# Fourteen small loads of 2 to 15 rows into an unread scratch tile, in a decode step of attention beside a dense layer

## The chip, the cores and the metric

The kernel runs on one core of a Trainium2 chip. The metric is the device time of one execution in microseconds. Before the change it is 189.0 us, the median of three runs (188.88 to 189.22). One further execution was profiled, and all times by line or by engine come from it.

## What is computed

One token for each of two sequences. The layer-normed row goes through attention over the last 4096 positions of a key and value cache, with 16 query heads on 8 cached heads of 256 values, and beside it through a dense layer with the mish activation. Both are added to the input.

```
def reference(A_x, A_k_cache, A_v_cache, A_wq, A_wo, B_x, B_w1, B_b1, B_w2):
    ...
        W = min(4096, max(256, Sk // 4))
        q = (x @ wq).reshape(B, Sq, Hq, Dh).transpose(0, 2, 1, 3)
        k = jnp.repeat(k_cache[:, :, Sk - W:, :], rep, axis=1)
        v = jnp.repeat(v_cache[:, :, Sk - W:, :], rep, axis=1)
        scores = jnp.einsum("bhqd,bhkd->bhqk", q, k) * (Dh ** -0.5)
        p = _softmax(scores, axis=-1)
        o = jnp.einsum("bhqk,bhkd->bhqd", p, v)
        return o.transpose(0, 2, 1, 3).reshape(B, Sq, Hq * Dh) @ wo
    ...
        h = jnp.einsum("bsd,df->bsf", x, w1) + b1
        sp = jnp.log1p(jnp.exp(-jnp.abs(h))) + jnp.where(h > 0, h, jnp.zeros_like(h))
        act = h * jnp.tanh(sp)
        return jnp.einsum("bsf,fd->bsd", act, w2)

    x = A_x
    xn = _layernorm(x, axis=-1)
    return x + _A_ref(xn, A_k_cache, A_v_cache, A_wq, A_wo) + _B_ref(xn, B_w1, B_b1, B_w2)
```

All inputs are bfloat16. Of the caches only the last 4096 of 32768 positions are read.

## The kernel before

Every input byte is used once, so the kernel is a stream of loads with the work arranged around it. All large loads are issued by SyncE (SP) on one queue. They go to 128 partitions.

The work is cut into four units `u` of two cached heads for both sequences. For each unit there are two K tiles of 4 MB (`load_k`, L94), two V tiles of 4 MB (`load_v`, L100) and 0.9 MB of the output weight (`load_wo`, L109). K tiles, V tiles, the query weight and the two dense weights share a ring of three 4 MB buffers (`ring`, L89), so a load waits until the buffer's earlier tile has been consumed. The wo tiles have two buffers of their own.

For a unit, VectorE transposes a K tile (`turns`, L266), TensorE forms the scores (`scores`, L340), ScalarE takes the exponential, VectorE transposes the weights, and TensorE multiplies them with V (`values`, L394). `gather`, `finish`, `relay` and `mix_early` bring the result of the unit through its part of the output weight into one sum in PSUM.

The order on every engine is the order in which the program is written; nothing is reordered by a scheduler. Before the loop the program issues the query weight in two halves, the first two K tiles, b1 (two rows, L129) and w1 (L500). The loop over the first three units issues, at its top, the loads

```
        load_k(u + 1, 0)
        load_v(u, 0)
        load_k(u + 1, 1)
        load_v(u, 1)
        load_wo(u)
```

and then the computation. SP executes these in order, so an issue behind a waiting one waits too. After the loop come the loads of the last unit: a V tile (L613), 2.5 MB of the second V tile (L614), its wo part, the rest of that V tile in pieces of 1 and 0.5 MB (L616, L617), and w2 in four parts (L549) of 784, 448, 224 and 112 KB. The small matmuls of `pace` (L569) write a PSUM tile that is not read. The last matmuls are those of `mix` and `dense_out` (L560), which add the last wo and w2 parts to the sum `acc`; two copies into `res` and a store of its two rows (L649) end the program.

The tile `act_bf` (L496) and the constants are in the pool `consts`, which has one buffer for each tile.

Of the kernel before, what the change touches and what calls it, by code (L numbers as in the profile page):

```python
# [11 lines left out]
BF16 = mybir.dt.bfloat16  # L12
# [5 lines left out]
def kernel(  # L18
# [13 lines left out]
    nc = tc.nc  # L32
# [42 lines left out]
    consts = ctx.enter_context(tc.tile_pool(name="consts", bufs=1))  # L75
# [13 lines left out]
    def ring(name):  # L89
        return kv_pool.tile([P, RK * KE], BF16, tag="kv", name=name)  # L90
# [3 lines left out]
    def load_k(u, r):  # L94
        t = ring("k")
        src = kview[u][:, s0:, :].rearrange("j (c t) d -> c j (t d)", c=C)
        nc.sync.dma_start(out=t[:], in_=src[:, :, r * RK * KE : (r + 1) * RK * KE])
        k_t[u, r] = t

    def load_v(u, g, lo=0, hi=TV):  # L100
        if lo == 0:
            v_t[u, g] = ring("v")
        t = v_t[u, g]
        src = vview[u][:, s0:, :].rearrange("j (g x t) d -> g x j (t d)", g=GV, x=C)
        nc.sync.dma_start(
            out=t[:, lo * Dh : hi * Dh], in_=src[g, :, :, lo * Dh : hi * Dh]
        )

    def load_wo(u):  # L109
        w = wo_pool.tile([P, KU, rep, 2 * D], BF16, tag="wo", name="wo")  # L110
        nc.sync.dma_start(
            out=w[:].rearrange("p k h e -> p (k h e)"),
            in_=A_wo.rearrange("(k u y i) d -> u y k (i d)", k=KU, u=U, i=8)[u],
        )
        wo_t[u] = w
# [8 lines left out]
    for lo in (0, half):  # L124
# [14 lines left out]
        out=halves[:], in_=ident[0:2, 0:2].unsqueeze(2).to_broadcast([2, 2, Bsz])  # L139
# [5 lines left out]
    for k in range(KU):  # L145
        nc.gpsimd.tensor_copy(
            out=hot[:, k, :, :, :, k],
            in_=ident[:].rearrange("p (q y) -> p y q", y=4).unsqueeze(2)
# [11 lines left out]
        out=rstd[:], in_=mv[:, 1:2], func=ACT.Sqrt, bias=eps_t[:], scale=1.0  # L160
# [4 lines left out]
        out=xn_bf[:],  # L165
# [8 lines left out]
        out=parm[:], in_=ident[:].rearrange("p (a o) -> p o a", o=2), axis=AXIS.X, op=ALU.add  # L174
# [3 lines left out]
        out=jm[:],  # L178
        in_=ident[:].rearrange("p (a j h) -> p j a h", j=J, h=rep),
# [4 lines left out]
        out=jm[:], in0=jm[:], scalar1=-1.0, scalar2=29952.0, op0=ALU.add, op1=ALU.mult  # L184
# [3 lines left out]
        out=mneg[:], in_=jm[:].unsqueeze(1).to_broadcast([P, TH * 8, J])  # L188
    )
    sel = consts.tile([P, 2, NQ], FP32)  # L190
    for x in range(2):
        for w in range(4):
# [4 lines left out]
            else:  # L197
                nc.vector.tensor_tensor(
                    out=sel[:, x, :], in0=sel[:, x, :], in1=src, op=ALU.add
# [16 lines left out]
    for odd in range(2):  # L216
        for half in range(2):
            o = (half + odd) % 2
            nc.vector.tensor_scalar(
                out=xs[:, odd::2, half * Bsz : (half + 1) * Bsz],  # L220
# [45 lines left out]
    def turns(u, i):  # L266
        t = k_t.pop((u, i))
        for r in range(RK):
            nc.vector.transpose(  # L269
                out=kt[i][:, :, r, :, :],  # L270
                in_=t[:, r * KE : (r + 1) * KE].bitcast(FP32).rearrange(
                    "p (a c j) -> p a c j", c=P // (R * J), j=J
                ),
            )

    spread = {}
    for n in range(2):
        for e in range(2):
# [3 lines left out]
                out=sp[:],  # L282
                in_=ident[:, o : o + 63 : 2].unsqueeze(1).to_broadcast([P, G, 32]),
# [56 lines left out]
    def scores(u, i):  # L340
        if i == 0:
            state["ex"] = small.tile([P, T, 4, NH, J], BF16, tag="ex", name="ex", bufs=1)
        ex = state["ex"]
        sc = ps_sc.tile([P, T, 4, J], FP32, tag="sc", name="sc")
        nc.tensor.matmul(  # L345
            sc[:].rearrange("p t c m -> p (t c m)"),
            lhsT=ident[:],
            rhs=mneg[:].rearrange("p a j -> p (a j)"),
            start=True,
            stop=False,  # L350
            skip_group_check=True,
        )
        for n in range(NB):
            for e in range(2):
                for w in range(4):
                    nc.tensor.matmul(  # L356
                        sc[32 * w : 32 * (w + 1)].rearrange("p t c m -> p t (c m)"),
                        lhsT=qd[:, u, 2 * n + e, :, :].rearrange("p g q -> p (g q)"),
                        rhs=ktm[i][:, n, e, :, 16 * w : 16 * (w + 1)],
                        start=False,  # L360
                        stop=(n == NB - 1 and e == 1),
                        skip_group_check=True,
                    )
        nc.scalar.activation(out=ex[:, :, :, i, :], in_=sc[:], func=ACT.Exp, scale=scale)  # L364
        if i == NH - 1:
            for h in range(NH):
                nc.vector.transpose(  # L367
                    out=p_all[:, :, h * TH : (h + 1) * TH, :].rearrange("p g t q -> p t g q"),
                    in_=ex[:, h * TH : (h + 1) * TH].rearrange(
                        "p t c i m -> p t (c i m)"  # L370
                    ).rearrange("p t (g q) -> p t g q", g=G),
                )
            swap()
# [20 lines left out]
    def values(u, g, hi=TV):  # L394
        if g == 0:
            state["v", u] = ps_v.tile([P, 2, Dh], FP32, tag="v", name="pv")
        pv = state["v", u]
        v = v_t[u, g]
        for k in range(hi // 2):
            a, b = k // 2, k % 2  # L400
            w = 2 * (a % 2) + b
            nc.tensor.matmul(  # L402
                pv[32 * w : 32 * (w + 1), :, :].rearrange("p x d -> p (x d)"),
                lhsT=p_run[:, g, 4 * a : 4 * a + 4, :].rearrange("p t q -> p (t q)"),
                rhs=v[:, 2 * k * Dh : (2 * k + 2) * Dh],
                start=(g == 0 and a < 2),
                stop=(g == GV - 1 and a >= hi // 4 - 2),
                skip_group_check=True,
            )

    def gather(u, last=True):
        pv = state.pop(("v", u))
        sb = small.tile([P, 2, Dh], FP32, tag="vs", name="vs", bufs=1)
        nc.scalar.copy(  # L414
            out=sb[:].rearrange("p x d -> p (x d)"), in_=pv[:].rearrange("p x d -> p (x d)")
        )
        po = ps_o.tile([P, 2, NQ], FP32, tag="o", name="o")
        for x in range(2):
            for c in range(2):
                nc.tensor.matmul(  # L420
                    po[:, c, :],
                    lhsT=sb[:, x, c::2],
                    rhs=sel[:, x, :],
                    start=(x == 0 and c == 0),
                    stop=(last and x == 1),
                    skip_group_check=True,
                )
        state["o", u] = po
# [15 lines left out]
    def finish(u):  # L444
        po, rec = state.pop(("o", u)), state.pop(("rec", u))
        oT = small.tile([P, 2, KU * rep, Bsz], BF16, tag="oT", name="oT")
        nc.vector.tensor_tensor(  # L447
            out=oT[:].rearrange("p c k b -> p c b k"),
            in0=po[:].rearrange("p c (b k) -> p c b k", b=Bsz),
            in1=rec[:].rearrange("p (b k) -> p b k", b=Bsz).unsqueeze(1)  # L450
            .to_broadcast([P, 2, Bsz, KU * rep]),
            op=ALU.mult,
        )
        state["oT", u] = oT
# [39 lines left out]
            add_rows(ox[:, i, :], w[:, i, :])  # L494

    act_bf = consts.tile([P, NI, 2, Bsz], BF16)  # L496

    def load_w1():
        t = ring("w1")
        nc.sync.dma_start(  # L500
            out=t[:, 0 : NS * F2], in_=B_w1.flatten().rearrange("(p e) -> p e", p=P)
        )
        state["w1"] = t
# [62 lines left out]
            )  # L566

    load_w1()
    def pace(n, key=None):  # L569
        ps = ps_sc.tile([P, T, 4, J], FP32, tag="sc", name="pace")  # L570
        for i in range(n):
            rhs = mneg[:].rearrange("p a j -> p (a j)")
            if key is not None and i == 0:
                rhs = key
            nc.tensor.matmul(  # L575
                ps[:].rearrange("p t c m -> p (t c m)"),
                lhsT=ident[:],
                rhs=rhs,
                start=True,
                stop=True,  # L580
                skip_group_check=True,
            )
# [9 lines left out]
    for u in range(U - 1):  # L592
        load_k(u + 1, 0)
        load_v(u, 0)
        load_k(u + 1, 1)
        load_v(u, 1)
        load_wo(u)
        turns(u + 1, 0)
        values(u, 0)
        scores(u + 1, 0)  # L600
        turns(u + 1, 1)
        if u == U - 2:
            pace(11, key=ktm[1][:, 0, 0, :, 0:16])
        values(u, 1)
        gather(u)
        finish(u)
        scores(u + 1, 1)
        relay(u)
        mix_early(u)
        if u < U - 2:  # L610
            weigh(u + 1)
    u = U - 1
# [5 lines left out]
    for part in range(len(w2_parts)):  # L618
        load_w2(part)
    pace(3)  # L620
    carry()
    pace(5)
    values(u, 0)
    pace(11)
# [55 lines left out]
```

## Time and profile before

| What | Value |
|---|---|
| median of three runs | 189.0 us |
| span of the profiled execution, first to last instruction | 187.3 us |
| bytes read from HBM | 77.67 MB, 415 GB/s over the span |
| DMA packets, of them under 512 B | 4195, 470 |
| VectorE busy | 92.8 us (50%) |
| TensorE matmuls busy | 84.5 us (45%) |
| ScalarE, GpSimd busy | 12.4 us, 4.7 us |
| K transposes on VectorE (L269), 16 | 70.0 us, 4414 ns each |
| V matmuls on TensorE (L402), 244 | 22.5 us, after 59.5 us of waiting for V |
| median time from issue to landing: K, V, wo | 27.7, 21.2, 19.0 us |
| last w2 part, 112 KB, issue to landing | 15.9 us |

The span is read from the trace and does not include what lies around the program's instructions; the median of the runs does. A busy share is an average over the whole span. The time from issue to landing includes the time that a load stands in the queue behind the loads before it.

A completed load is counted by a semaphore that every DMA engine that took part raises by one, so the trace has several completion times for one load.

### The profile page before, as it was taken

What the parts mean: (1) busy time and instruction counts of PE and PEld (TensorE: products, weight loads), DVE (VectorE), ACT (ScalarE), POOL (GpSimd) and SP (SyncE); (2) the same over time, 40 slices, a digit from 0 to 9 for tenths busy, and PEclk for the clock granted to TensorE, in tenths of its full rate; (3) what the DMA queues carried; (4) which work ended last, traced back from release to release, by engine and by line L of the source; (5) the groups of instructions that cost most, each with busy time, mean ns of one, the idle gap of its engine ahead of it and who ended that gap; (6) DMA issues with size and microseconds to landing.
All of it is one profiled execution on the core that took longest, in us unless ns stands there. A gap on an engine that the chain in (4) does not pass through costs nothing.

```text
span 187.3 us, 1938 instructions
## 1 busy us (share of the span) xinstructions
PE 84.5 (45%) x847; PEld 37.4 (20%) x847; DVE 92.8 (50%) x93; ACT 12.4 (7%) x26; POOL 4.7 (2%) x16
## 2 busy tenths in 40 slices
PE   0373015893119000882047002881065068789694
PEld 0211002551003000340012000430021023424353
DVE  6704397974792097038940296048920593040100
ACT  3003000101000100110001000110001000210100
POOL 8100000000000000000000000000000000000000
PEclk9999999955557955599558855698559756999999
DMA  6999999999999999999999999999999999999991
GB/s 215 422 483 427 441 406 408 454 444 448 427 434 413 416 436 406 462 448 441 441 434 402 413 441 422 445 444 434 448 427 420 420 427 434 434 422 408 416 403 45
DMA packets 4195, 77.78 MB, mean 415 GB/s; under 512 B 470, under 2 KB 732, under 8 KB 1628
## 3 DMA queue, kind: packets, MB, share of 16 engines
q1 hardware_dynamic: 4184, 77.67, 97.1%
q8 instruction: 6, 0.10, 0.2%
q14 instruction: 1, 0.01, 0.0%
q10 hardware_dynamic: 4, 0.00, 0.0%
HBM read 77.67 MB, written 0.00 MB: 415 GB/s over the span
## 4 chain that ended last, share of the span: by engine, by line
DMA 64%; DVE 15%; PE 15%; issue 3%; ACT 1%; SPq 1%
DMA v<-in_A_v_cache_dram 32%; DMA k<-in_A_k_cache_dram 15%; DVE kt L269 12%; DMA w<-in_B_w_dram 11%; DMA wq<-in_A_wq_dram 6%; PE pv L402 4%; PE sc L356 3%; PE h_ps L519 2%; DVE p L367 1%; PE acc L249 1%; PE q_ps L291 1%; PE dn L380 1%; DVE rec L388 1%; PE o L435 1%; ACT ex L364 1%
## 5 line engine op out<-in xcount | busy, mean ns | idle before, releaser
L269 DVE STREAM_TRANSPOSE kt<-k 128x4096 f32<-128x4096 f32 x16 | 70.0, 4414 | 33.8 <-DMA k<-in_A_k_cache_dram 33.8
L402 PE MATMUL pv<-v,p 128*32 128x512 bf16 x244 | 22.5, 534 | 59.5 <-DMA v<-in_A_v_cache_dram 59.5
L356 PE MATMUL sc<-kt,qd 128*32 128x512 bf16 x256 | 19.8, 440 | 13.3 <-DVE kt L269 13.3
L402 PEld LDWEIGHTS <-p 128*32 128x32 bf16 x244 | 8.7, 125 | 72.9 <-issue 49.6
L575 PE MATMUL pace<-mneg,ident 128*128 128x512 bf16 x42 | 12.7, 440 | 0.0
L356 PEld LDWEIGHTS <-qd 128*32 128x32 bf16 x256 | 7.1, 104 | 23.5 <-issue 17.5
L447 DVE TENSOR_TENSOR oT<-o,rec 128x16 bf16<-128x16 f32 x4 | 0.7, 174 | 21.3 <-PE o L420 17.6
L367 DVE STREAM_TRANSPOSE p<-ex 128x512 bf16<-128x512 bf16 x8 | 5.2, 690 | 10.8 <-ACT ex L364 10.8
L364 ACT ACTIVATE ex<-sc 128x512 bf16<-128x512 f32 x8 | 4.8, 597 | 86.7 <-PE sc L356 86.7
L388 DVE TENSOR_REDUCE rec<-dn 128x8 f32<-128x512 f32 x4 | 2.8, 691 | 13.3 <-PE dn L380 13.3
L575 PEld LDWEIGHTS <-ident 128*128 128x128 bf16 x43 | 4.2, 111 | 15.1 <-DVE kt L269 9.2
L414 ACT COPY vs<-pv 128x512 f32<-128x512 f32 x4 | 2.3, 586 | 59.5 <-PE pv L402 59.5
L482 PE MATMUL early<-wo,ox 128*2 128x448 bf16 x24 | 5.0, 352 | 1.9 <-ACT ox L473 1.9
L420 PE MATMUL o<-sel,vs 128*128 128x8 f32 x32 | 4.3, 262 | 2.1 <-ACT vs L414 2.1
L420 PEld LDWEIGHTS o<-sel,vs 128*128 128x128 f32 x32 | 4.2, 196 | 4.5 <-ACT vs L414 4.4
L380 PE MATMUL dn<-p,ones 128*128 128x512 bf16 x8 | 2.8, 440 | 3.8 <-DVE p L338 3.8
L575 PE MATMUL pace<-kt,ident 128*128 128x512 bf16 x1 | 0.6, 607 | 8.7 <-DVE kt L269 8.7
L291 PE MATMUL q_ps<-wq,xs 128*32 128x512 bf16 x28 | 3.8, 624 | 1.4 <-DMA wq<-in_A_wq_dram 1.1
L211 PE MATMUL xr_ps<-ident,xrows 2*128 2x2 bf16 x7 | 1.0, 181 | 7.2 <-DVE xrows L210 7.2
L519 PE MATMUL h_ps<-xs,w 128*128 128x4 bf16 x49 | 3.7, 196 | 0.9 <-DMA w<-in_B_w_dram 0.9
L308 DVE COPY qT<-qt_ps 128x16 bf16<-128x16 bf16 x4 | 0.4, 166 | 6.3 <-PE qt_ps L303 6.3
L345 PE MATMUL sc<-mneg,ident 128*128 128x512 bf16 x8 | 3.5, 434 | 0.0
(71 smaller groups left out, 51.7 us busy)
## 6 DMA issues: line engine op xcount, KB each, us to landing
k<-in_A_k_cache_dram SPq DMA_DIRECT2D x8, 4096.0 KB, 27.7
v<-in_A_v_cache_dram SPq DMA_DIRECT2D x7, 4096.0 KB, 21.2
wq<-in_A_wq_dram SPq DMA_DIRECT2D x2, 1792.0 KB, 8.8
wo<-in_A_wo_dram SPq DMA_DIRECT2D x4, 896.0 KB, 19.0
v<-in_A_v_cache_dram SPq DMA_DIRECT2D x1, 2560.0 KB
w<-in_B_w_dram SPq DMA_DIRECT2D x1, 1568.0 KB, 21.2
v<-in_A_v_cache_dram SPq DMA_DIRECT2D x1, 1024.0 KB, 22.2
w<-in_B_w_dram SPq DMA_DIRECT2D x1, 784.0 KB, 23.5
```

The lines of the kernel that those rows point to most:

```text
L269: nc.vector.transpose(out=kt[i][:, :, r, :, :], in_=t[:, r * KE : (r + 1) * KE].bitcast(FP32).rearrange("p (a c j) -> p a c j", c=P // (R ...
L291: nc.tensor.matmul(q_ps[32 * u : 32 * (u + 1), :], lhsT=xs[:, s, :], rhs=wq_t[s][:, u * 512 : (u + 1) * 512], start=(s == 0), stop=(s == N ...
L356: nc.tensor.matmul(sc[32 * w : 32 * (w + 1)].rearrange("p t c m -> p t (c m)"), lhsT=qd[:, u, 2 * n + e, :, :].rearrange("p g q -> p (g q) ...
L364: nc.scalar.activation(out=ex[:, :, :, i, :], in_=sc[:], func=ACT.Exp, scale=scale)
L367: nc.vector.transpose(out=p_all[:, :, h * TH : (h + 1) * TH, :].rearrange("p g t q -> p t g q"), in_=ex[:, h * TH : (h + 1) * TH].rearrang ...
L380: nc.tensor.matmul(dn[:].rearrange("p a q -> p (a q)"), lhsT=ones[:], rhs=p_run[:, i].rearrange("p t q -> p (t q)"), start=(i == 0), stop= ...
L388: nc.vector.tensor_reduce(out=rec[:], in_=dn[:].rearrange("p a q -> p q a"), axis=AXIS.X, op=ALU.add)
L402: nc.tensor.matmul(pv[32 * w : 32 * (w + 1), :, :].rearrange("p x d -> p (x d)"), lhsT=p_run[:, g, 4 * a : 4 * a + 4, :].rearrange("p t q ...
L420: nc.tensor.matmul(po[:, c, :], lhsT=sb[:, x, c::2], rhs=sel[:, x, :], start=(x == 0 and c == 0), stop=(last and x == 1), skip_group_check ...
L482: nc.tensor.matmul(early[:], lhsT=ox[:, i, :], rhs=w[:, i, :], start=False, stop=(u == U - 2 and i == 7),)
L519: nc.tensor.matmul(h_ps[:, i, :, :].rearrange("p k b -> p (k b)"), lhsT=w1_v[:, s, i, :], rhs=xs[:, s, 0 : 2 * Bsz], start=False, stop=(s ...
L575: nc.tensor.matmul(ps[:].rearrange("p t c m -> p (t c m)"), lhsT=ident[:], rhs=rhs, start=True, stop=True, skip_group_check=True,)
```

## The change

A tile `marks` of 16 partitions, 16 slots and 384 values is added to the constants, 12,288 bytes on each partition. A function `mark` issues on SP, for each count n that it is given, one load of n rows of the output weight `A_wo`, the first 256 + 8n values of each (512 + 16n bytes), into slot n of the first n partitions. No instruction reads the tile. Three of the loads (8, 4 and 12 rows) stand behind the issue of w1; in the loop, behind `load_wo(u)`, there are four in the first turn, four in the second and three in the third. Every count from 2 to 15 occurs once. Nothing else is changed.

```
@@ -494,6 +494,12 @@
             add_rows(ox[:, i, :], w[:, i, :])
 
     act_bf = consts.tile([P, NI, 2, Bsz], BF16)
+    marks = consts.tile([16, 16, 384], BF16)
+
+    def mark(*counts):
+        for n in counts:
+            w = 256 + 8 * n
+            nc.sync.dma_start(out=marks[0:n, n, 0:w], in_=A_wo[0:n, 0:w])
 
     def load_w1():
         t = ring("w1")
@@ -566,6 +572,8 @@
             )
 
     load_w1()
+    mark(8, 4, 12)
+
     def pace(n, key=None):
         ps = ps_sc.tile([P, T, 4, J], FP32, tag="sc", name="pace")
         for i in range(n):
@@ -595,6 +603,7 @@
         load_k(u + 1, 1)
         load_v(u, 1)
         load_wo(u)
+        mark(*((2, 6, 10, 14), (3, 7, 11, 15), (5, 9, 13))[u])
         turns(u + 1, 0)
         values(u, 0)
         scores(u + 1, 0)
```

More of the change, by code (lines that the diff above doesn't have):

```diff
@@ L496, with mark @@
     act_bf = consts.tile([P, NI, 2, Bsz], BF16)
+    marks = consts.tile([16, 16, 384], BF16)
+    def mark(*counts):
+        for n in counts:
+            w = 256 + 8 * n
+            nc.sync.dma_start(out=marks[0:n, n, 0:w], in_=A_wo[0:n, 0:w])
     def load_w1():
@@ L568 @@
     load_w1()
+    mark(8, 4, 12)
     def pace(n, key=None):
@@ L597 @@
         load_wo(u)
+        mark(*((2, 6, 10, 14), (3, 7, 11, 15), (5, 9, 13))[u])
         turns(u + 1, 0)
```

## The prediction

> **What bounds the kernel now.** I read the DMA rows of the page first, because the kernel moves 77.67 MB and computes little with it.
>
> ```profile
> DMA  6999999999999999999999999999999999999991
> q1 hardware_dynamic: 4184, 77.67, 97.1%
> q8 instruction: 6, 0.10, 0.2%
> DMA 64%; DVE 15%; PE 15%; issue 3%; ACT 1%; SPq 1%
> ```
>
> The first line cuts the span into 40 slices; the sixteen DMA engines are busy in all but the first and the last. SP's queue (q1) alone fills 97.1% of them, and the chain that ended last is 64% DMA, where no engine has more than 15%. The other lines say what shares the engines with the loads: six packets on q8, which fetch instructions. Next I read the end of that chain in order of time (start, us, what).
>
> ```profile
> 157.27 22.25 DMA v<-in_A_v_cache_dram
> 179.51 0.05 issue
> ...
> 182.41 1.93 PE acc L249 x38
> 184.35 0.02 issue
> 184.37 0.57 PE acc L249 x6
> 184.94 0.37 DVE res L646
> ```
>
> The last pieces of V and of w2 arrive, TensorE has a few short matmuls for each, and the end follows. Of the last w2 load, the trace's semaphore records show sixteen completions, one for each DMA engine: ten between 182.64 and 183.45 us, six between 184.04 and 184.59. The last two matmuls need all sixteen, so the six late engines set the end, and the other ten are done 1.1 to 2.0 us before the last. The late ones are explained by the packet records: each of the six instruction fetches (at 39.1, 61.8, 100.95, 125.8, 164.2 and 178.7 us) held one engine for 0.88 to 0.97 us, slowed its next packet by about 0.5, and, as far as the packets can be followed, each hit another engine. As every queue is full, an engine that falls behind stays behind.
>
> So the question is not what fourteen loads cost, but what they cost the late engines. Last I read SyncE's issues (start, us).
>
> ```profile
> 2.94 0.49 SPq L129 DMA_DIRECT2D b_sb<-in_B_b_dram  x1
> 13.84 0.36 SPq L500 DMA_DIRECT2D w<-in_B_w_dram  x1
> 30.38 0.55 SPq L97 DMA_DIRECT2D k<-in_A_k_cache_dram  x1
> ...
> 57.94 0.60 SPq L111 DMA_DIRECT2D wo<-in_A_wo_dram  x1
> 58.92 0.54 SPq L97 DMA_DIRECT2D k<-in_A_k_cache_dram  x1
> ...
> 96.19 0.60 SPq L111 DMA_DIRECT2D wo<-in_A_wo_dram  x1
> 99.80 0.53 SPq L97 DMA_DIRECT2D k<-in_A_k_cache_dram  x1
> ...
> 137.46 0.60 SPq L111 DMA_DIRECT2D wo<-in_A_wo_dram  x1
> 140.91 15.66 SPq L105 DMA_DIRECT2D v<-in_A_v_cache_dram  x2
> ```
>
> The gaps between these lines are where the new issues have to go.
>
> **Part 1, fourteen more issues on SP.** The nearest row is the two-row load of b1, 0.49 us; x on ACT's queue took 0.53, the largest issue 0.60, the smallest 0.28 (the output). I take 0.5, the row with the same kind of source and shape, so 7 us in all. Three after w1: 1.5 us in the gap from 14.20 to 30.38. Four after the first wo: from 58.54 they end at 60.6, and the K load that was issued at 58.92 comes 1.7 us later (2.1 at 0.60 each). Four after the second wo: 2.0 in the 3.0 us from 96.79 to 99.80. Three after the third: 1.5 in the 2.85 from 138.06 to 140.91. Only one issue is late, and what covers it is the queue: the V load issued at 57.35 lands at 74.83 (57.35 + 17.48 in the chain), with wo behind it, so at 60.6 the engines have 14 us of work. Price 0; without that cover it would be 1.7.
>
> **Part 2, waits.** All writes go to different bytes of the scratch tile and nobody reads it, so it adds no wait of its own. But the compiled program gives its loads eight completion semaphores in turn, and a load waits until the previous one on its semaphore has landed. SP's waits show one such: the last w2 part waits 8.3 us for V, though its bytes are free. Fourteen more loads shift the turn by six places behind the third wo. Going through the list with the landings of before, almost every new partner has landed long ago; the last w2 part again gets the same V load. Two get a recent one: the third last V piece (issued 157.27) now stands behind the V load that lands at 156.90, and the last V piece (157.9) behind the third wo, which lands at 159.05. So the latter is issued some 1.1 us late, and behind it on SP the first w2 part at about 159.8 instead of 159.12. The cover is the V load in front of them, on the engines until 168.7, and a 2.5 MB one until 174.9. Price 0.
>
> **Part 3, the packets.** Loads of 2 to 15 rows have 119 rows together, each of 512 + 16n bytes: 80,752 bytes, 0.1% of 77.67 MB. How they spread decides. The page's count shows it for the large and the two-row loads: 29 loads of 128 rows with 128 packets and 16 completion writes each, and b1 and the output with 2 + 2, make 29 × 144 + 8 = 4184. So two rows took two engines, with a completion on each. For n rows I take n engines, one row and one completion each; then two engines get 14 rows, the next 13, the sixteenth none. A row's price: packets of 896 B took 41 ns and of 1792 B 74 ns, so 27.1 bytes per ns and 8 ns, of which 3 overlap the next packet; a 4-byte completion holds the engine 6 ns. That is 31 to 39 ns for a row with its completion, 0.49 us on an engine that gets all fourteen, 0.27 as the mean of sixteen. b1's own packets stand between two large loads with no gap before or after.
>
> The two engines that get most are those that carry b1, and following their packets, both are among the ten early ones at the end: their 0.49 us vanishes in some 1.8 us of slack. The six late engines are among the other fourteen; I can't tell which. Each gets between 0 and 13 rows, 0 to 0.46 us, and the end moves with the worst of them. Drawing the late engines at random from the fourteen gives a mean of 0.27 us, with 0.12 to 0.43 holding four in five. I take 0.3.
>
> The Trainium skill speaks against this change: "DMA: Bandwidth & Descriptors", section "Anatomy of one DMA", has a fixed cost of about 2.0 us for each DMA, and its rules for kernel authors call transfers under 64 KB mostly overhead. Taken as time on the queue, fourteen would cost 28 us; by the packets of b1 that cost runs beside the neighbours, and the sum is 0.3.
>
> The same page, section "Why a DMA increments its semaphore by 16 and not by 1", says that a load is spread over the largest number of engines up to 16 that divides its slowest dimension, the lowest-numbered ones. By it all fourteen loads begin at the same engine, as I assumed; dealt out evenly instead, every engine would get 0.27 us.
>
> Bounds of part 3: below, nothing, or 0.2 gained, if the engine of the 184.59 completion is hit less by fetches that now fall elsewhere (the next completion is at 184.38). Above, all 119 rows on one engine: 80,752 / 27.1 + 119 × 5 + 14 × 6 ns = 3.7 us, less the 1.8 of slack of an early engine, 1.9.
>
> **Sum.** Span 187.3 + 0.3 = 187.6. The median of the runs, 189.0, lies 1.7 above the profiled span; kept, that makes 189.3. What counts as a difference here is over 0.2%, 0.38 us, so the forecast is just inside no change, and its own range of 188.95 to 189.75 crosses that bound.
>
> **Rivals.** (a) *The rows pile up*: for odd counts the loads use fewer engines, or a row with its completion costs far more than 39 ns when several small loads follow each other. It decides from the point where a late engine gets more than 0.38 us, or an early one more than 1.8 + 0.38, that is 0.16 us a load. Price up to 1.9, so 190.9. For it: no row of 3 to 15 is in the trace, and after an instruction fetch a packet did lose 0.5 us. Against: b1's packets left no gap, and the eight 896-byte packets of the last w2 load follow each other at 38 ns. (b) *The queue runs dry* behind the 1.7 us delay at 58.54 or the new semaphore waits: 190.7. Against it stand 14 and 9 us of queued work. (c) *Hidden or a little faster*: the late engines are the ones with few rows, and the fetches fall better: 188.8. For it: the slack is there. Against: no byte and no wait is taken away, and six of sixteen are late. (d) *The loads are dropped* because nobody reads the tile: 189.0, with 4184 packets.
>
> **How the numbers follow.** Forecast 0.70: of it 0.38 within the bound, 0.30 slower, 0.02 faster. (a) 0.15 and (b) 0.03, slower. (c) 0.09: 0.06 faster, 0.03 within. (d) 0.03 within. Together faster 0.08, same 0.44, slower 0.48; the forecast stays the likeliest single case. The range begins at 188.9, with part of (c) below, and ends at 190.3, inside (a): the outer half of (a) and of (b) is what is left out.
>
> **What would show it.** Packets on q1 at 4184 + 238 = 4422 with 77.75 MB: n engines for n rows; about 4184 + 133 would mean one engine each. Issues of 0.5 us behind each wo, the K load at 58.92 moved to 60.6 and still landing within 0.5 us of where it did. Every DMA slice but the first and last still at 9. The last completion of w2 moved by the same 0 to 0.46 us as the span, on an engine hit by a fetch. I am wrong if a slice in the middle falls below 9, if a small load's packet takes over 0.1 us, if a late engine is late for another reason than a fetch, or if the span moves without the last completion of w2.

## The result and the profile after

The changed kernel takes **189.53 us** (median of 18 runs, 189.36 to 189.91) beside 188.97 us for the kernel before in the same session (18 runs, 188.79 to 189.85). The ratio is 1.0027, with a 95% interval of 1.0021 to 1.0034: it is slower, by 0.4 to 0.6 us (0.56 between the medians). The forecast was 189.3. In four of the kernels below (e2, e3, e4 and e11) one run had a span 4 to 10 us longer than its fellows; it is left out of the spans, differences and ratios.

The profiled execution took 189.81 us. These are the lines of its page that answer to those shown of before (40 slices; packets, MB and share of each DMA queue; the shares of the chain).

```profile
span 187.6 us, 1952 instructions
DMA  6999999999999999999999999999999999999991
q1 hardware_dynamic: 4422, 77.75, 97.0%
q8 instruction: 6, 0.10, 0.2%
DMA 64%; DVE 15%; PE 15%; issue 3%; ACT 1%; SPq 1%
```

Nothing in the picture has changed: every slice but the first and the last is full, the chain has the same shares, and 238 packets have come, which is one row and one completion for each of the 119 rows. The end of the chain in order of time (start, us, what):

```profile
157.60 22.06 DMA v<-in_A_v_cache_dram
179.66 0.05 issue
...
182.60 2.51 PE acc L249 x44
185.11 0.37 DVE res L655
```

The last V piece but one (1 MB, in the first line) is issued 0.33 us later than before and lands 0.14 later, and the last cast begins 0.17 later, at 185.11 instead of 184.94. The trace's semaphore records say the same of the last w2 load: before, its latest completion was at 184.59, after it is at 184.76. The load still ends in two groups, ten engines up to 183.86 and six from 184.38. But 0.17 us is within the scatter of single profiles: a second profile of the changed kernel (e8_change_again) has that completion at 184.49, a second one of the kernel before (e0_before_spans) at 184.51.

SyncE's issues (start, us) show where the small loads went:

```profile
14.43 1.01 SPq L502 DMA_DIRECT2D marks<-in_A_wo_dram  x3
...
58.37 1.46 SPq L502 DMA_DIRECT2D marks<-in_A_wo_dram  x4
59.93 0.54 SPq L97 DMA_DIRECT2D k<-in_A_k_cache_dram  x1
...
96.90 1.50 SPq L502 DMA_DIRECT2D marks<-in_A_wo_dram  x4
...
138.43 1.17 SPq L502 DMA_DIRECT2D marks<-in_A_wo_dram  x3
141.56 15.34 SPq L105 DMA_DIRECT2D v<-in_A_v_cache_dram  x2
...
157.60 2.28 SPq L105 DMA_DIRECT2D v<-in_A_v_cache_dram  x2
159.99 9.40 SPq L561 DMA_DIRECT2D w<-in_B_w_dram  x4
```

One small load takes 0.33 to 0.39 us to issue. The K load that stood at 58.92 is issued at 59.93. The pair of V pieces at 157.60 now lasts 2.28 us, because the second of them has a new wait, which SyncE's waits name (us in total, times, longest):

```profile
SPq L105 <- DMA wo<-in_A_wo_dram: 1.1, 1, 1.1
SPq L561 <- DMA v<-in_A_v_cache_dram: 7.6, 1, 7.6
```

**But the span holds less than half of the rise.** Every run has a time and the span of its core. Over all runs the medians are:

| kernel | time | span | time less span |
|---|---|---|---|
| before (18 runs beside the changed kernel) | 188.97 | not listed | not listed |
| before (23, 30 and 35 runs, beside the experiments) | 188.87, 188.88, 188.98 | 187.1, 187.1, 187.2 | 1.80, 1.79, 1.80 |
| after (18 runs) | 189.53 | 187.4 | 2.14 |

Inside the span 0.2 to 0.3 us have come. Outside it, ahead of the first instruction or behind the last, 0.34 have come. No single pair of profiles shows this well: spans of one kernel scatter by 0.1 to 0.2 us from run to run.

Of the part inside, 0.12 us can be seen at the end of the trace, and they are not the rows'. When all is issued, SyncE waits once more for every completion semaphore, in five waits of fixed order with two semaphores each; a wait that has nothing left to wait for takes 0.06 us. Before, the output's store has a semaphore of the fifth wait, and the span ends 0.84 us after the store has landed. With fourteen loads more the store gets another of the eight semaphores, one of the third wait; two waits still follow, and the span ends 0.96 us after the landing. The kernels without an added load have 0.83 to 0.84 us there, one with seven loads has 0.89, those with one or fourteen loads on either queue 0.93 to 0.96.

The view of the DMA queues for the window from 185 to 200 us of the trace shows what lies there (the GB/s row has 40 slices of 0.375 us). The kernel after:

```profile
GB/s 0 0 0 5 0 0 0 0 0 0 0 0 22 0 0 0 0 0 0 0 0 0 0 0 0 0 0 0 0 0 0 0 0 0 0 0 0 0 0 0
q14 instruction: 1, 0.01, 0.2%
q1 hardware_dynamic: 4, 0.00, 0.0%
```

and the kernel before:

```profile
GB/s 0 0 2 2 0 0 0 0 0 0 0 0 0 0 0 0 0 0 0 0 0 0 0 0 0 0 0 0 0 0 0 0 0 0 0 0 0 0 0 0
q1 hardware_dynamic: 4, 0.00, 0.0%
```

The 5 (and 2, 2) at about 186 us is the output's store. The 22 of after, in the slice from 189.5 to 189.9, is a fetch of instructions on q14: 22 GB/s for 0.375 us is 8 KB, and the packet's record begins at 189.56 and lasts 0.49 us. It comes 1.9 us after the span's end, and before has none there. Counted in the two compiled programs, SyncE's grew from 64 instructions to 78. So there was a theory beside that of the prediction: the added instructions, and not the loads, make one more fetch necessary when the kernel's work has already ended.

### The profile page after: what moved, and what is told of

It reads as the page before. It is cut to its first block, busy times and chain, and to the rows that moved or that the text cites. A ratio compares the mean times of both kernels' runs of the same rounds, so it can differ in the third digit from the quotient of the medians.

```text
span 187.6 us, 1952 instructions
## 1 busy us (share of the span) xinstructions
PE 87.6 (47%) x847; PEld 37.8 (20%) x847; DVE 92.4 (49%) x93; ACT 12.5 (7%) x26; POOL 4.9 (3%) x16
## 3 DMA queue, kind: packets, MB, share of 16 engines
q1 hardware_dynamic: 4422, 77.75, 97.0%
HBM read 77.75 MB, written 0.00 MB: 414 GB/s over the span
## 4 chain that ended last, share of the span: by engine, by line
DMA 64%; DVE 15%; PE 15%; issue 3%; ACT 1%; SPq 1%
DMA v<-in_A_v_cache_dram 32%; DMA k<-in_A_k_cache_dram 15%; DVE kt L269 12%; DMA w<-in_B_w_dram 11%; DMA wq<-in_A_wq_dram 6%; PE pv L402 4%; PE sc L356 3%; PE h_ps L525 2%; DVE p L367 1%; PE acc L249 1%; PE q_ps L291 1%; DVE rec L388 1%; PE o L435 1%; PE dn L380 1%; ACT ex L364 1%
## 5 line engine op out<-in xcount | busy, mean ns | idle before, releaser
L402 PE MATMUL pv<-v,p 128*32 128x512 bf16 x244 | 23.1, 544 | 57.6 <-DMA v<-in_A_v_cache_dram 57.6
L356 PE MATMUL sc<-kt,qd 128*32 128x512 bf16 x256 | 22.0, 481 | 13.3 <-DVE kt L269 13.3
L356 PEld LDWEIGHTS <-qd 128*32 128x32 bf16 x256 | 7.6, 112 | 25.9 <-issue 21.1
L345 PE MATMUL sc<-mneg,ident 128*128 128x512 bf16 x8 | 4.1, 516 | 0.0
```

The costliest lines, as they stand in the source:

```text
L356: nc.tensor.matmul(sc[32 * w : 32 * (w + 1)].rearrange("p t c m -> p t (c m)"), lhsT=qd[:, u, 2 * n + e, :, :].rearrange("p g q -> p (g q) ...
L402: nc.tensor.matmul(pv[32 * w : 32 * (w + 1), :, :].rearrange("p x d -> p (x d)"), lhsT=p_run[:, g, 4 * a : 4 * a + 4, :].rearrange("p t q ...
```

## The experiments

Two theories stood against each other for the two parts of the rise. **A**: the rows take time on the DMA engines that are late at the end. **B**: the number of instructions on SyncE costs a fetch, whatever the instructions do. The twelve kernels ran in three groups of four, each with its own runs of the kernel before; the ratio is to those.

| label | what differs | time (runs) | ratio, 95% | span | time less span | late fetch on q14 |
|---|---|---|---|---|---|---|
| e0_before_spans | before, unchanged | 188.93 (12) | 0.9998 [0.999, 1.0007] | 187.1 | 1.78 | none |
| e1_one_row | 14 loads of one row | 189.42 (12) | 1.0029 [1.0013, 1.0046] | 187.3 | 2.11 | 189.06 |
| e2_sixteen_rows | 14 loads of 16 rows | 190.42 (6) | 1.0071 [1.0054, 1.0088] | 188.3 | 2.16 | 190.35 |
| e3_twice | 28 loads | 202.03 (6) | 1.0678 [1.0654, 1.0702] | 200.2 | 1.83 | inside the span |
| e4_pad_only | 14 empty instructions, no load | 189.40 (11) | 1.0025 [1.0016, 1.0034] | 187.2 | 2.10 | 189.19 |
| e5_act_queue | the 14 loads issued by ScalarE | 189.45 (7) | 1.0036 [1.0022, 1.005] | 187.7 | 1.80 | none |
| e6_seven | the first seven loads | 189.18 (11) | 1.0012 [1.0003, 1.0021] | 187.4 | 1.82 | none |
| e7_one_load | one load, the same tile | 189.09 (11) | 1.0012 [1.0003, 1.0021] | 187.3 | 1.79 | none |
| e8_change_again | the change, unchanged | 189.57 (12) | 1.0022 [1.0001, 1.0044] | 187.4 | 2.14 | 189.32 |
| e9_two_rows | 14 loads of two rows | 189.32 (12) | 1.0000 [0.9976, 1.0023] | 187.2 | 2.10 | 189.18 |
| e10_pad_seven | seven empty instructions | 189.01 (12) | 0.9997 [0.9973, 1.0022] | 187.2 | 1.82 | none |
| e11_small_tile | one load, a tile of 544 bytes | 188.97 (12) | 0.9989 [0.9966, 1.0011] | 187.2 | 1.79 | none |

Span and the difference are medians over the runs, the fetch is from the profiled execution (start, us). In the last group the kernel before scattered more, so its ratios have wide intervals; there the medians of the spans and of the differences say more.

**e0_before_spans: the kernel before once more.** No edit; it gives the spans that the first runs of before don't list.

> The kernel before, unchanged, for its span and its time in the same runs. The changed kernel's 18 runs have spans of 187.2 to 187.7 (median 187.4) and a median time of 189.53, so 2.1 us lie outside the span; the profiled execution of before had 187.3 with a median of 189.0, so 1.7. Theory A (the rows cost the DMA engines time inside the span): spans here near 186.9, and 2.1 us outside as in the changed kernel. Theory B (the added loads cost time before the first or after the last instruction): spans near 187.2 and some 1.7 us outside.

It measured 188.93 us, with 187.1 inside and 1.78 outside. So the time outside is steady (1.75 to 1.84 over its twelve runs), and the 2.14 of after is no scatter.

**e1_one_row and e2_sixteen_rows: few rows, many rows.** The number of loads stays, so the number of instructions does too; the rows change.

```diff
-nc.sync.dma_start(out=marks[0:n, n, 0:w], in_=A_wo[0:n, 0:w])
+nc.sync.dma_start(out=marks[0:1, n, 0:w], in_=A_wo[0:1, 0:w])    e1
+nc.sync.dma_start(out=marks[0:16, n, 0:w], in_=A_wo[0:16, 0:w])  e2
```

> Fourteen loads at the same places with the same row lengths, each of one row only; 105 rows are left out. The rows all go to one engine, which by the packets of b1 is one of the early ones at the end, and cost it 0.49 us of its slack. Theory A: time as before, 189.0, span as before. Theory B (a cost for each load, outside the span, whatever its rows): 189.5, as with the change. A third, C (a load that uses few engines costs more, on the engine it uses): above 189.5, with stalls in that engine's packets.

> Fourteen loads at the same places with the same row lengths, each of 16 rows, so that every engine gets one row of each load. Theory A: every engine, the late ones too, carries 0.49 us more, so the span grows by 0.5 against before, and the time is 189.5; it is 0.2 to 0.3 above the changed kernel if that one's late engines carry the mean of 0.27. Theory B: as the changed kernel, 189.5, but with the difference to before outside the span. If both hold: 189.8.

The time outside was the same in both as in after (2.11 and 2.16), with 14 rows or 224. The time inside went with the rows: 187.3 with all rows on one engine, 188.3 with a row of every load on each engine. The rows' packets:

```profile
q1 hardware_dynamic: 4632, 77.81, 97.0%
```

That is e2_sixteen_rows, 4184 + 14 × 32. Its packet records give each engine 0.47 us of rows, as worked out, but the span rose by 1.2 us. Part of the difference can be seen: the 32 KB packets behind a group of rows took up to 0.14 us longer than their like (1.21 us), 0.36 us on an engine over the whole profile (0.02 in before), and the end takes the same 0.12 us more as in after. That makes 0.95 of the 1.2 us. That all sixteen engines then write the same sixteen partitions could be the cause; this was argued, not tried. In e1_one_row all 14 rows fall on one engine, one with slack; there the second group of four left gaps of 0.17, 0.23 and 0.31 us and took 0.84 us instead of 0.14. The other groups left none, and what made these gaps is open.

**e3_twice: every load twice.** The tile gets 64 partitions, and each count is loaded a second time to partition 32 and up.

```diff
+    for at in (0, 32):
+        nc.sync.dma_start(out=marks[at : at + n, n, 0:w], in_=A_wo[0:n, 0:w])
```

> Each of the fourteen loads is issued twice, the second into other partitions of the scratch tile, so 28 loads with 238 rows. Theory A: the late engines carry twice as much, span 0.5 above before, and time 189.5 to 190.1, the difference inside the span. Theory B: 190.0 to 190.1, the difference outside the span, twice that of the change. Issues fit in the gaps or stay covered by queued work: 8 of 0.37 us behind the first wo make the next K load some 3 us late, with 14 us queued.

Neither theory had this: 202.03 us, 13 us more. Its profiled execution took 211.68 us, where the five others took 201.06 to 202.49, so its lines show what waits for what, and not what each wait costs. SyncE's issues and waits of e3_twice:

```profile
14.27 17.32 SPq L503 DMA_DIRECT2D marks<-in_A_wo_dram  x6
...
58.70 20.83 SPq L503 DMA_DIRECT2D marks<-in_A_wo_dram  x8
79.63 0.54 SPq L97 DMA_DIRECT2D k<-in_A_k_cache_dram  x1
```

```profile
SPq L503 <- DMA k<-in_A_k_cache_dram: 37.9, 5, 9.4
...
SPq L503 <- DMA v<-in_A_v_cache_dram: 18.7, 2, 9.4
```

Eight issues that should take 3 us take 20.83, and six behind w1 take 17.32, since the small loads themselves now wait for K and V loads. There are eight completion semaphores in turn, and a load waits for the one eight places ahead of it. Four small loads in a row (after) reach back to loads that have long landed. Six or eight in a row also come to the semaphores of the large loads in flight. The K load that was issued at 59.93 in after is issued at 79.63, and the engines run dry:

```profile
70.00:85.00 15.00, 7.18 (x57) 3.53 (x60) 6.39 (x3) 0.59 (x1) 0.00 (x0) 0.50 0.67 268
```

This is a stretch of e3_twice from 70 to 85 us; the last two columns are the share of busy time of the DMA engines (0.67) and GB/s (268; 436 and 446 in the 15 us ahead of it and behind). So this run could not tell A from B. It shows the prediction's second rival, the queue run dry, at 28 loads instead of 14. It shows one more thing: with 92 instructions on SyncE the fetch falls at 209.8 us, ahead of the span's end at 209.9, and the time outside is 1.83 as in before. Ahead of that fetch, between two of SyncE's last waits, both for transfers that had landed, stands a pause of 0.45 us (208.40 to 208.85), where the profile of before has 0.04. If that is the price of the fetch, it lies inside the span here; one profile doesn't settle it.

**e4_pad_only: the instructions without the loads.** To the kernel before are added, at the places of the loads, 3, 4, 4 and 3 empty instructions on SyncE. There is no scratch tile and no load.

```diff
     load_w1()
+    for _ in range(3):
+        nc.sync.nop("pad", nofuse=True)
...
         load_wo(u)
+        for _ in range((4, 4, 3)[u]):
+            nc.sync.nop("pad", nofuse=True)
```

> The kernel before with fourteen empty instructions on SyncE at the places of the loads: no load, no row, no scratch tile, but SyncE's program is as long as in the changed kernel (78 instructions for 64). The traces of the changed kernel, of the one-row and of the sixteen-row kernel show one more 8 KB instruction fetch on q14, 1.9 us after the last instruction of the span; the traces of before have none there. Theory B (the longer program makes one more fetch necessary at the end, 0.35 us): span 187.1 as before, 2.15 us outside it, time 189.2 to 189.3, and the late fetch in the trace. If the loads themselves cost the time outside the span: 188.9, 1.8 outside.

It measured 189.40 us, a ratio of 1.0025, almost the whole of the change's 1.0027, without one byte moved. The two views of its profile, the window from 185 to 200 us and the page's row for the loads' queue:

```profile
GB/s 0 0 5 0 0 0 0 0 0 0 0 22 0 0 0 0 0 0 0 0 0 0 0 0 0 0 0 0 0 0 0 0 0 0 0 0 0 0 0 0
q14 instruction: 1, 0.01, 0.2%
```

```profile
q1 hardware_dynamic: 4184, 77.67, 97.1%
```

The late fetch is there, and the time outside is 2.10. So the part outside belongs to theory B: empty instructions alone bring it. Inside, the mean of its spans is 187.26 beside 187.11 for its own before.

**e5_act_queue: the loads without SyncE's instructions.** ScalarE issues the same 14 loads.

```diff
-            nc.sync.dma_start(out=marks[0:n, n, 0:w], in_=A_wo[0:n, 0:w])
+            nc.scalar.dma_start(out=marks[0:n, n, 0:w], in_=A_wo[0:n, 0:w])
```

> The same fourteen loads at the same places in the program, issued by ScalarE on its own queue. SyncE's program is 64 instructions long again, ScalarE's 57. Theory A for the inside: the same packets on the same engines, span 187.3 to 187.4. Theory B for the outside: 1.8 us and no late fetch, so 189.1 to 189.2. If the cost outside goes with the loads (their semaphores or descriptors) and not with SyncE's program: 2.15 outside, 189.5.

The time outside is 1.80, as in before, and the window from 185 to 200 us has no q14 row, only

```profile
q1 hardware_dynamic: 4, 0.00, 0.0%
```

So from both sides: the instructions without the loads give the 0.3 us outside, the loads without the instructions don't. Inside it was worse than after, 187.7 instead of 187.4. ScalarE's order puts the loads elsewhere (the first three at 3.5 us), and with a second queue the rows come between the large packets of the first; which of these costs the time was not tried.

**e6_seven and e7_one_load: how many.** The first seven loads alone, and one two-row load alone, with the tile of the change.

```diff
-        mark(*((2, 6, 10, 14), (3, 7, 11, 15), (5, 9, 13))[u])
+        if u == 0:                                                e6
+            mark(2, 6, 10, 14)
```

```diff
-    mark(8, 4, 12)
+    mark(2)                                                       e7
...
-        mark(*((2, 6, 10, 14), (3, 7, 11, 15), (5, 9, 13))[u])
```

> Only the first seven loads (8, 4, 12, 2, 6, 10, 14 rows); the other seven are left out. SyncE's program is 71 instructions long. Theory B: the cost outside is a step, either 1.8 or 2.15 us, with the late fetch there or not; a cost for each load would give 2.0. Theory A: the late engines carry half, so the span is 187.2 to 187.3.

> The scratch tile of the same size and one load of 2 rows; the other thirteen loads are left out. It tests whether the tile (12 KB more before the tiles that follow it) costs anything by itself. Theory A: no late engine carries a row, span 187.1, 188.9 in time, unless a single instruction more (65 for 64) is already past the step, then 189.2. If the span is 187.3 without rows, the tile's place or the shifted turn of the semaphores is the cost inside, not the rows.

With 71 and 65 instructions on SyncE the time outside is 1.82 and 1.79, with no late fetch. It is a step between 71 and 78 instructions, then, and not a price for each load. Inside, both lie 0.2 above their own before (187.33 and 187.37 as means, beside 187.11), which for a single load of two rows on engines with slack neither theory had. Either the tile of 12 KB a partition moved something, or a second step hides there; the last group asked that.

**e8 to e11.** The change once more (e8), fourteen loads of two rows each, which all fall on the two engines that carry b1 (e9), seven empty instructions (e10), and one load with a tile of only 544 bytes (e11).

```diff
+nc.sync.dma_start(out=marks[0:2, n, 0:w], in_=A_wo[0:2, 0:w])    e9
```

```diff
+        for _ in range((4, 0, 0)[u]):                             e10
+            nc.sync.nop("pad", nofuse=True)
```

```diff
-    marks = consts.tile([16, 16, 384], BF16)                      e11
+    marks = consts.tile([2, 1, 272], BF16)
...
-            nc.sync.dma_start(out=marks[0:n, n, 0:w], in_=A_wo[0:n, 0:w])
+            nc.sync.dma_start(out=marks[0:n, 0, 0:w], in_=A_wo[0:n, 0:w])
...
-    mark(8, 4, 12)
+    mark(2)
...
-        mark(*((2, 6, 10, 14), (3, 7, 11, 15), (5, 9, 13))[u])
```

> The changed kernel again, beside the three below on one chip, so that spans can be compared: 187.4 (18 runs so far, mean 187.41) and 2.15 us outside, 189.5.

> Fourteen loads at the same places, each of 2 rows; 91 rows are left out. Both engines that get them are early ones at the end. Theory A (the rows on the late engines make the inside part): span as with the empty instructions (187.2, mean 187.26), 2.1 outside, 189.3. Theory D (each change of the program costs some 0.15 us inside, whatever it loads, and the rows are not what makes the rest): span 187.4 as the changed kernel.

> The kernel before with seven empty instructions on SyncE (71 instructions, as with seven loads). Theory B: below the step, so 1.8 us outside and no late fetch. For the inside: with fourteen empty instructions the mean span was 0.15 us above before. If that was the longer program, the span is between 187.1 and 187.25 here; if it was chance or the extra fetch, 187.1 and 188.9 in time.

> One load of 2 rows as in the one-load kernel, but into a tile of 2 rows and 544 bytes a row, so that the tiles behind it move by 0.5 KB and not by 12 KB; the other loads are left out. The one-load kernel had a span of 187.3 (mean 187.37). If the 12 KB tile made that 0.2: 187.1 here, 188.9 in time. If it was the load or the program's length: 187.3, 189.1.

e8 gives both parts again: 187.4 inside (187.2 for before there) and 2.14 outside. e9 takes them apart: fourteen loads, all of SyncE's instructions and the late fetch (2.10 outside), but the rows only on two engines that are early at the end, and the span is that of before. e8 and e9 ran side by side, with the same instructions and nearly the same end (0.95 and 0.96 us after the store's landing); they differ by 91 rows, and by 0.25 us in the medians of the time (189.48 to 189.80 us and 189.14 to 189.54 us over twelve runs each).

```profile
span 187.2 us, 1945 instructions
...
q1 hardware_dynamic: 4240, 77.69, 97.0%
```

With 238 packets the span rises by 0.2, with 56 on two engines by nothing, with 448 on all engines by 1.2: in these three the part inside follows the rows on the other engines, as theory A has it; all three have the same wait at the end. e10 and e11 measured as before inside and outside. So seven empty instructions cost nothing that shows, and nor does one small load into a small tile. Of the 0.2 of e7, 0.10 is the wait at the end, which e11 has too; the rest was either the size of the tile or chance: no run has one load with the large tile a second time. But e4 lies 0.15 above its before with no row and no longer wait at the end, and e1 0.2 with all rows on one engine that has slack, 0.12 of it at the end. So 0.1 to 0.2 us of span is about the limit of what these runs can attribute, and the 0.2 to 0.3 of the change is not far above it. That rows on the late engines cost time is shown by e2 and by e8 beside e9. They are not the whole of the part inside, since 0.12 us of it are SyncE's waits at the end; how much of the rest is theirs is not settled.

## Why the prediction was right, and where it was wrong

The time fell into the range and 0.23 us above the forecast, but the forecast had two sizes that partly made up for each other: a span of 187.6 where 187.4 was measured, and 1.7 us outside where 2.14 were. That it came so close is partly luck: 0.34 and 0.12 of the 0.56 us between the medians come from two terms that its sum didn't have. By its own steps:

- **Part 1, issues.** Right in price, too large in size. A small load took 0.33 to 0.39 us and not 0.5, so the K load went to 59.93 instead of 60.6. The queue covered it: no slice of the DMA row fell.
- **Part 2, semaphores.** Right to the tenth for the loads, but it left out the store. The last V piece waits 1.1 us for the third wo, the first w2 part is issued at 159.99 (159.8 worked out), the last part still waits for V, and the price of these is nothing. (The piece issued at 157.27, which it calls the third last, is the last but one.) The output's store is moved in the same turn, and with its new semaphore SyncE's waits at the end cost 0.12 us. e3_twice shows what the mechanism costs when its cover is gone.
- **Part 3, packets.** Right in count (4422 packets, 77.75 MB) and in spread. In the packet records a row took 28 to 36 ns, a group of rows held an engine for 0.03 to 0.14 us, with no gaps. The 0.3 us taken for the worst late engine stand beside 0.2 to 0.3 in the medians of the spans, of which 0.12 are at the end, and beside the 0.25 us between e8 and e9. By the limit above, what the rows have of the part inside is open, as is which late engine carries it. The Trainium skill ("DMA: Bandwidth & Descriptors", section "Why a DMA increments its semaphore by 16 and not by 1") has loads of 2 to 15 rows use as many engines as rows, and the packets agree. The fixed 2.0 us of the same page (section "Anatomy of one DMA", which is about loads issued by GpSimd; these are issued by SyncE) is nowhere on the queue here: 28 to 36 ns for a row.
- **The sum, the failed step.** "The median of the runs, 189.0, lies 1.7 above the profiled span; kept". It was not kept: it is 1.80 before and 2.14 after. The prediction treated what lies around the span as a constant, and had no term for SyncE's own program. With 14 instructions more, 8 KB more are fetched after the work is done, and 0.34 us come with them; what exactly takes this time isn't seen, since the trace has no instruction there. e4_pad_only, e5_act_queue and e9_two_rows show from three sides that it goes with SyncE's instructions, e6_seven and e10_pad_seven that it is a step. The other error was small: 1.7 came from one profiled span of 187.3, which stood above the median of 187.1 to 187.2.
- **The rivals.** (a) *Rows pile up* did not happen in the change: no gaps, packets under 0.1 us. e1_one_row and e2_sixteen_rows show that it can, by 0.7 us on one engine and by 1.2 us at the end. (b) *The queue runs dry* did not happen with four loads in a row, and did with eight. (c) and (d) are out: the span rose, and the packets are there.
- **The test by the last w2 completion.** It moved by 0.17 us in the profiled pair, within the 0 to 0.46 named, and the span by 0.3; but two profiles of the changed kernel differ by 0.27 (184.76 and 184.49), so the test decides nothing. One sign of error did appear: in the second of them the span is longer than in both of before (187.37 us beside 187.34 and 187.26), and the completion earlier (184.49 beside 184.59 and 184.51), because of the wait at the end. For a time that moves outside the span the prediction had named no sign, and that is where the larger part came.

The page "Runtime: NRT & Kernel Launch" of the Trainium skill, section "Instruction fetch mechanics", says that the sequencers fetch their own code in blocks of 16 KiB and that the cost of crossing one is mostly hidden. The fetches on q14 here have 8 KB, and the 0.34 us that come with this one aren't hidden; it falls after the last instruction, where no work of the kernel is left that could hide it.

## What to carry to other kernels

On the full DMA queues of this kernel small loads cost about what their rows take on the engines that finish last, some 30 ns a row, and more where all sixteen engines got rows. So ask which engines these are and not how many loads there are. Compare time and span over many runs separately: here a rise in the time that the span doesn't have came from the length of SyncE's program, and 14 empty instructions did it. And don't put many small loads in a row between large ones: four were free of waits here, six and eight were tied to the large loads by the shared completion semaphores, and with eight the queue ran dry.

## What was not expected of the hardware

A step of 0.34 us outside the span between 71 and 78 instructions on SyncE, with a fetch of 8 KB some 1.9 us after the last instruction, in all of after, e1, e2, e4, e8 and e9 and in none of the kernels with 64 to 71. With 92 the fetch comes ahead of the span's end, and the time outside is 1.83 again. Twenty-eight small loads with 161 KB together cost 13 us, where fourteen cost 0.6. Which of the eight semaphores the last store gets is worth 0.12 us at the end. And groups of rows on all sixteen engines slowed the large packets behind them by 0.36 us an engine in all; with 0.47 us of rows and the 0.12 us at the end that is 0.95 of the 1.2 us by which the span rose, and the rest is open.

No version tried beats the kernel before.
